# Attention and a cosine feed-forward on one core: weights decoded in pairs, the first tile cut in two around the second, and the start laid out by due times

## The chip, the core and the metric

The kernel runs on one core of a Trainium2 chip. TensorE (PE) multiplies, ScalarE (ACT) and VectorE (DVE) work on elements, GpSimd (POOL) does a few odd jobs, SyncE (SP) issues the DMAs. The metric is device time of one execution in microseconds (us); lower is better.

## What is computed

```
# q, k: random normals of about 0.573, v: 0.1; each (8, 8, 576, 64)
scores = scale * matmul(q_c, k_c^T)        # blocks of 64 positions, 9 in a sequence
attn = exp(scores - max); attn /= sum + 1e-9
x = matmul(attn, v_c)  ->  (4608, 512)     # heads side by side
h = x @ w_in                               # (512, 2048)
out = (h * cos(h)) @ w_out                 # (2048, 512)
```

The weights arrive as 64-bit floats and are decoded to 32-bit floats on the chip. Each large product is made in three passes of a fast 32-bit type: every operand is split in a rounded part ("hi") and the rest ("lo"), and hi x hi, hi x lo and lo x hi are added up.

## The kernel before

The 4608 tokens are 9 tiles of 512. w_in and w_out are cut along the 2048 inner columns in 16 blocks of 128 each; `("in", fc)` and `("out", fc)` name them. The kernel goes through 9 x 16 steps. In step s of tile t, `hidden(t, fc)` multiplies the tile's x with block fc of w_in (12 matmuls of 128x512 into PSUM bank h), `activate` makes g = h cos(h) from it in six instructions that go to and fro between ACT and DVE (whole turns on ACT, what is over on DVE, sine on ACT, product with h on DVE, g_hi on ACT, g_lo on DVE), and `project`, three steps behind (`LAG = 3`), adds g times block fc of w_out to four PSUM banks acc0 to acc3 (12 matmuls again). After a tile's last block the four banks are copied out (`finish`) and stored. There are two banks for h, so `hidden` of step s + 2 waits until the product with h of step s is done.

Attention of the next tile is made during a tile: `scores`, maximum, difference, exponential, sum, inverse, quotient, a transposition and `weighted`, whose result is split in the hi and lo parts of x. On PE these are four groups for a tile (two of scores, two of weighted values), two head pairs hp at a time. For tile 0 all of it comes before the first step; for tile 1 it is done in tile 0's steps in another form (`attend_early`), with the quotients on POOL.

Weights: `load_weight` brings a block of 512 KB to a room `w_in0`, `w_out0` and so on. `split_weight` decodes it. A double's upper 16 bits go into "half words" (magnitude: Abs; scale: Relu with factor 8, both on ACT; sign: or-ed in on DVE), its next 32 bits into a tile w (low: Relu on ACT), xor on DVE puts the two together, high (a copy on ACT) rounds, and rest (subtraction on DVE) gives the lo part. The lines from magnitude to xor, in this order magnitude, scale, low, sign, xor:

```
            half, low = half_words[(name == "out")], w.bitcast(U32)
            hb = half[:, :, 1]
            nc.scalar.activation(hb.bitcast(BF16), top.bitcast(BF16), AF.Abs)
            nc.scalar.activation(hb, hb, AF.Relu, bias=float(7 - (MORE << 7)), scale=8.0)
            nc.scalar.activation(low, mid, AF.Relu, bias=float((1 << 19) - 1), scale=-(2.0**-13))
            nc.vector.scalar_tensor_tensor(
                hb, top, 0x8000, hb, op0=ALU.bitwise_and, op1=ALU.bitwise_or
            )
            nc.vector.tensor_tensor(
                low, low, half.rearrange("p n k -> p (n k)").bitcast(U32), op=ALU.bitwise_xor
            )
```

So w_in blocks and w_out blocks each have a room of half words of their own (`half0`, `half1`). Two blocks of each kind are decoded ahead (`AHEAD = 2`).

Order: the instructions of tile 0's steps and of everything ahead of them are put in order on each engine by the framework's scheduler; from tile 1 on `keep_in_program_order` holds each engine to the order of the code, in which the queues `soon`, `late` and `full` place attention pieces behind parts of `activate`. Every engine works through its own instructions in order.

## Time and profile before

| | |
|---|---|
| time, median of 3 runs | 880.68 us (880.52 to 880.91) |
| time of the profiled execution | 880.95 us |
| its span, first to last instruction | 879.1 us |
| PE busy | 853.0 us (97%) |
| weight loads of PE (PEld) | 697.1 us (79%) |
| DVE busy | 576.7 us (66%) |
| ACT busy | 407.9 us (46%) |
| POOL busy | 5.5 us (1%) |
| moved by DMA | 55.42 MB, 63 GB/s over the span |

The profile is one execution on the chip. Busy shares are means over stages with different limits, so they are read by stretches of time; matmuls are pipelined, and a PE that is "busy" need not be at its best pace. The granted clock of TensorE has two levels, 1.2 GHz (0.50) and 2.4 GHz (1.00).

### The profile page before, as it was taken

The numbers are of one execution on the slowest core, as the hardware profiler recorded it, in microseconds if no ns is written. First come the engines' busy times: TensorE is split into PE (matmuls) and PEld (weight loads), VectorE is DVE, ScalarE is ACT, GpSimd is POOL, SyncE is SP. The second block draws the span as 40 slices with busy tenths as digits, with TensorE's granted clock in tenths as the row PEclk, the third lists the DMA queues.
The fourth block names the chain that finished last, engine by engine and source line by source line (L and its number), as shares of the span: only waits on it lengthen the run. The fifth ranks groups of instructions, "written<-read, shape, count | busy, mean of one in ns | idle before, by whom it ended". The sixth has DMA issues, their size and how long they took to land.

```text
span 879.1 us, 14100 instructions
## 1 busy us (share of the span) xinstructions
PE 853.0 (97%) x5792; PEld 697.1 (79%) x5792; DVE 576.7 (66%) x975; ACT 407.9 (46%) x660; POOL 5.5 (1%) x9
## 2 busy tenths in 40 slices
PE   4899999999999999999999999999999999999998
PEld 3587777888888888888888888888888888888886
DVE  5999986766577656764686558655766577644332
ACT  4998993533354335333533344333533354333332
POOL 0001000000000000000000000000000000000000
PEclk8599999999999999999999999999999999999999
DMA  9980013100310012001300040003100010001001
GB/s 346 406 340 33 14 25 110 47 26 25 96 49 25 24 49 96 25 1 50 120 1 25 25 145 1 25 25 97 49 25 25 1 48 25 1 1 48 1 1 48
DMA packets 25407, 55.42 MB, mean 63 GB/s; under 512 B 2816, under 2 KB 2816, under 8 KB 25344
## 3 DMA queue, kind: packets, MB, share of 16 engines
q1 hardware_dynamic: 25344, 54.54, 17.7%
q8 instruction: 45, 0.74, 0.4%
q14 instruction: 18, 0.15, 0.1%
HBM read 45.09 MB, written 9.44 MB: 62 GB/s over the span
## 4 chain that ended last, share of the span: by engine, by line
PE 85%; ACT 11%; DMA 1%; DVE 1%; issue 1%; SPq 0%; ACTq 0%
PE acc L74 41%; PE h L74 40%; PE a L74 4%; ACT half L124 2%; ACT half L125 2%; ACT w L126 2%; DMA w_out<-in_w_out_dram 1%; ACT g_hi L360 1%; ACT g L356 1%; ACT w_out L136 1%; ACT w_in L136 1%; ACT g L353 1%; DMA kt<-in_kT_dram 1%; ACT pts L270 0%; ACT x L321 0%
## 5 line engine op out<-in xcount | busy, mean ns | idle before, releaser
L74 PE MATMUL h<-x,w_in 128*128 128x512 f32 x1704 | 416.9, 393 | 5.9 <-ACT x L321 2.8
L74 PEld LDWEIGHTS h<-x,w_in 128*128 128x128 f32 x1704 | 321.1, 189 | 75.0 <-DVE g L357 4.5
L74 PE MATMUL acc<-w_out,g_hi 128*128 128x512 f32 x1152 | 355.2, 392 | 0.0
L74 PEld LDWEIGHTS acc<-w_out,g_hi 128*128 128x128 f32 x1152 | 214.0, 188 | 45.2
L74 PE MATMUL acc<-w_out,g_lo 128*128 128x512 f32 x576 | 221.1, 390 | 0.6 <-DVE g_lo L361 0.6
L354 DVE SCALAR_TENSOR_TENSOR g<-g,h 128x512 f32<-128x512 int32 x142 | 97.2, 684 | 138.3 <-ACT g L353 137.6
L353 ACT ACTIVATE g<-h 128x512 int32<-128x512 f32 x142 | 84.7, 596 | 190.1 <-PE h L74 190.1
L361 DVE TENSOR_TENSOR g_lo<-g,g_hi 128x512 fp32r<-128x512 f32 x144 | 102.5, 712 | 79.9 <-ACT g_hi L360 77.0
L356 ACT ACTIVATE g<-g 128x512 f32<-128x512 f32 x144 | 91.0, 632 | 128.2 <-DVE g L354 128.0
L360 ACT CAST g_hi<-g 128x512 fp32r<-128x512 f32 x144 | 89.3, 620 | 128.9 <-DVE g L357 79.3
L357 DVE TENSOR_TENSOR g<-h,g 128x512 f32<-128x512 f32 x142 | 98.1, 691 | 56.5 <-ACT g L356 53.0
L74 PEld LDWEIGHTS acc<-w_out,g_lo 128*128 128x128 f32 x576 | 108.1, 188 | 23.7 <-DVE g_lo L361 1.1
L282 DVE STREAM_TRANSPOSE pts<-e 32x256 f32<-32x256 f32 x224 | 97.4, 435 | 3.7
L125 ACT ACTIVATE half<-half 128x512 uint16<-128x512 uint16 x32 | 25.1, 786 | 0.2
L74 PEld LDWEIGHTS a<-kt,qt 64*64 64x64 f32 x1024 | 18.9, 135 | 7.6 <-issue 6.8
L130 DVE TENSOR_TENSOR w<-w,half 128x512 uint32<-128x512 uint32 x32 | 22.0, 687 | 1.8 <-ACT w L126 1.0
L74 PEld LDWEIGHTS a<-pts,vt 64*64 64x64 f32 x1024 | 16.6, 134 | 7.2 <-issue 5.3
L322 DVE TENSOR_TENSOR x<-a,x 128x512 fp32r<-128x512 f32 (+1 forms) x38 | 21.9, 614 | 0.1
L74 PE MATMUL a<-kt,qt 64*64 64x64 f32 x1024 | 21.8, 222 | 0.0
L74 PE MATMUL a<-pts,vt 64*64 64x64 f32 x1024 | 19.0, 222 | 0.7 <-ACT pts L270 0.7
L216 DVE TENSOR_TENSOR e<-a,m 128x512 f32<-128x512 f32 x28 | 19.2, 686 | 0.5
L212 DVE TENSOR_REDUCE m<-a 128x8 f32<-128x512 f32 x28 | 19.2, 684 | 0.0
(61 smaller groups left out, 316.5 us busy)
## 6 DMA issues: line engine op xcount, KB each, us to landing
qt<-in_qT_dram SPq DMA_DIRECT2D x36, 256.0 KB, 4.0
kt<-in_kT_dram SPq DMA_DIRECT2D x36, 256.0 KB, 4.2
vt<-in_v_dram SPq DMA_DIRECT2D x34, 256.0 KB, 3.0
w_in<-in_w_in_dram SPq DMA_DIRECT2D x16, 512.0 KB, 9.1
w_out<-in_w_out_dram SPq DMA_DIRECT2D x16, 512.0 KB, 9.4
out_dram<-w SPq DMA_DIRECT2D x16, 256.0 KB, 2.1
out_dram<-half SPq DMA_DIRECT2D x16, 256.0 KB, 2.0
out_dram<-x SPq DMA_DIRECT2D x4, 256.0 KB, 2.0
```

The lines of the kernel that those rows point to most:

```text
L74: kept(nc.tensor.matmul(*args, **kw))
L125: nc.scalar.activation(hb, hb, AF.Relu, bias=float(7 - (MORE << 7)), scale=8.0)
L130: nc.vector.tensor_tensor(low, low, half.rearrange("p n k -> p (n k)").bitcast(U32), op=ALU.bitwise_xor)
L212: kept(nc.vector.tensor_reduce(out=m, in_=sv, op=ALU.max, axis=AX.X))
L282: kept(nc.vector.transpose(out=dst[o : o + BL, :, qb], in_=src[i : i + BL, :, kb]))
L322: kept(nc.vector.tensor_tensor(lo, xq, hi.bitcast(F32), op=ALU.subtract))
L353: kept(nc.scalar.activation(n, h, AF.Identity, bias=0.25, scale=0.5 / math.pi))
L354: kept(nc.vector.scalar_tensor_tensor(g, n, -2.0 * math.pi, h, op0=ALU.mult, op1=ALU.add))
L356: kept(nc.scalar.activation(g, g, AF.Sin, bias=0.5 * math.pi))
L357: kept(nc.vector.tensor_tensor(g, h, g, op=ALU.mult))
L360: kept(nc.scalar.copy(out=g_hi, in_=g))
L361: kept(nc.vector.tensor_tensor(g_lo, g, g_hi.bitcast(F32), op=ALU.subtract))
```

## The change

Weights are loaded and decoded as pairs. A pair has one room of raw data, one tile w, and both its blocks pass each decoding instruction together (128x1024 elements instead of 128x512). There is one room of half words, for a pair, in place of two for a block. The pairs are, for the first eight and then for the last eight fc: (in, in) twice, (in, out) four times, (out, out) twice.

The order of steps is a list: tile 0 with fc 0 to 7, all of tile 1, tile 0 with fc 8 to 15, then tiles 2 to 8. The sums of tile 0's first half are copied from PSUM, stored to a DRAM buffer, and loaded again when tile 1 is out; DVE adds them to the second half's. Tile 2's attention falls in the second half of those first 32 steps (`STAGE`); its x take over tile 1's rooms (`x_room`, two sets of four, by parity).

All instructions are now held in program order. For the first 32 steps that order is made by the kernel: everything that one engine does is a piece (engine, length, what to run, pieces it comes after, time of a load), each piece gets a due time, going backwards from hidden and project blocks that follow each other from 23 us on, and a loop places next the piece that can start, by due time among those that can start within 0.2 us. Lengths in this list are constants of the source. Tile 1's four quotients and two of tile 0's are on POOL, one head pair at a time; exponentials of later tiles are two instructions of 1024 elements instead of one of 2048.

```diff
-    xp = ctx.enter_context(tc.tile_pool(name="xp", bufs=8))
+    xp = ctx.enter_context(tc.tile_pool(name="xp", bufs=4))
...
+    hbm = ctx.enter_context(tc.tile_pool(name="hbm", bufs=1, space=bass.MemoryType.DRAM))
...
-    ordered = False
-
     def kept(ins):
-        if ordered:
-            tc.keep_in_program_order(ins)
+        tc.keep_in_program_order(ins)
         return ins
...
-    half_words = []
-    for i in range(2):
-        half = wts.tile([P, TOK, 2], U16, name=f"half{i}")
...
+    half = wts.tile([P, 2, TOK, 2], U16, name="half")
...
+    def split_weights(pair):
...
+            pieces = [
+                lambda: kept(nc.scalar.activation(hb.bitcast(BF16), top.bitcast(BF16), AF.Abs)),
+                lambda: kept(nc.scalar.activation(hb, hb, AF.Relu, bias=more, scale=8.0)),
+                lambda: kept(nc.scalar.activation(
+                    w().bitcast(U32), mid, AF.Relu, bias=most, scale=-(2.0**-13)
+                )),
+                lambda: kept(nc.vector.scalar_tensor_tensor(
+                    hb, top, 0x8000, hb, op0=ALU.bitwise_and, op1=ALU.bitwise_or
+                )),
+                lambda: kept(nc.vector.tensor_tensor(
+                    w().bitcast(U32), w().bitcast(U32), words, op=ALU.bitwise_xor
+                )),
+            ]
...
+        def high():
+            parts = wts.tile([P, ROOM], F32R, name="w_%s%d_%s%d" % (*pair[0], *pair[1]))
+            made_parts.append(parts)
+            kept(nc.scalar.copy(out=beside(parts, at[0]), in_=w()))
...
+        def rest():
+            hi, lo = (beside(made_parts[0], at[0] + i * n) for i in range(2))
+            kept(nc.vector.tensor_tensor(lo, w(), hi.bitcast(F32), op=ALU.subtract))
...
+    def x_room(t, dtype):
+
+        return xp.tile([P, 2, TOK], dtype, name=f"x{(t + (t > 1)) % 2}")
...
+    order = [(0, fc) for fc in range(GROUP)] + [(1, fc) for fc in range(NFC)]
+    order += [(t, fc) for t in range(NT) if t != 1 for fc in range(0 if t else GROUP, NFC)]
...
+        if not whole:
+
+            os, to = att.tile([P, DM], F32, name="vt" if sub % 2 else "pts"), partial[sub]
+        elif t == 0:
+            os = acc["partial", sub]
...
+        if whole and t == 0:
+            kept(nc.vector.tensor_tensor(os, os, o, op=ALU.add))
...
+    for pair in pairs:
+        key = ("w", pair)
+        made[key] = split_weights(pair)
+        a = piece(ACT, 1.15, rest_of(key, 0), xored, at=here[pair])
+        r = piece(ACT, 1.15, rest_of(key, 1), a)
+        m = piece(ACT, 0.88, rest_of(key, 2), back[-2], at=here[pair])
+        g = piece(DVE, 1.19, rest_of(key, 3), r)
+        xored = piece(DVE, 1.13, rest_of(key, 4), m, g)
+        h = piece(ACT, 0.88, rest_of(key, 5), xored)
+        back.append(piece(DVE, 1.13, rest_of(key, 6), h))
...
+                if t or hp < 2:
+                    q[hp] = piece(POOL, 1.0, lambda hp=hp: quotient(t, hp, nc.gpsimd), i)
+                else:
+                    q[hp] = piece(DVE, 0.6, lambda hp=hp: quotient(t, hp), i)
...
+    for i in reversed(range(len(work))):
+        for a in work[i][3]:
+            due_at[a] = min(due_at[a], due_at[i] - work[a][5])
...
+                near = [
+                    (d if e != PE or work[i][1] > 2 else 0.0, start, i)
+                    for start, d, i in c if start <= soonest + 0.2
+                ]
+                d, start, i = min(near)
...
+    for start, i in sorted(starts):
+        work[i][2]()
+    for s in range(STAGE, len(order) + LAG):
...
```

Two places of the order on the engines show what the pairs do. The first is ACT in the middle of decoding. Before, in tile 0's steps (names end in buffer numbers; half0 and half1 are the two rooms of half words; L124 is the magnitude, L125 scale, L126 low, L136 high, L353 and L356 whole turns and sine, L360 g_hi):

```order
L136 CAST w_in5_710<-w_704 128x512
L124 ACTIVATE half0_87<-w_in6_158 128x512
L125 ACTIVATE half0_87<-half0_87 128x512
L360 CAST g_hi_534<-g_533 128x512
L353 ACTIVATE g_593<-a0_580 128x512
L126 ACTIVATE w_756<-w_in6_158 128x512
L136 CAST w_out5_719<-w_713 128x512
L124 ACTIVATE half1_89<-w_out6_160 128x512
L125 ACTIVATE half1_89<-half1_89 128x512
L356 ACTIVATE g_593<-g_593 128x512
```

After, around the pairs (in4, out0) and (in5, out1) (L136 is the magnitude, L137 scale, L138 low, L161 high, L388, L390 and L392 belong to the activation):

```order
L161 CAST w_in4_out0_573<-w_470 128x2x512
L136 ACTIVATE half_89<-w_in5_out1_143 128x1024
L137 ACTIVATE half_89<-half_89 128x1024
L388 ACTIVATE g_595<-h_548 128x512
L392 CAST g_hi_562<-g_561 128x512
L138 ACTIVATE w_618<-w_in6_out2_146 128x1024
L390 ACTIVATE g_595<-g_595 128x512
L161 CAST w_in5_out1_631<-w_567 128x2x512
L136 ACTIVATE half_89<-w_in6_out2_146 128x1024
L137 ACTIVATE half_89<-half_89 128x1024
```

Before, the magnitude of out6 goes to the other room right after that of in6; after, each magnitude stands behind the high of the pair before it and writes the same room `half_89`.

The second place is DVE at the same stretch. Before (L127 sign, L130 xor, L137 rest, L354, L357 and L361 the activation):

```order
L130 TENSOR_TENSOR w_756<-w_756,half0_87 128x512
L137 TENSOR_TENSOR w_out5_719<-w_713,w_out5_719 128x512
L127 SCALAR_TENSOR_TENSOR half1_89<-w_out6_160,half1_89 128x512
L357 TENSOR_TENSOR g_593<-a0_580,g_593 128x512
L354 SCALAR_TENSOR_TENSOR g_653<-g_653,a1_640 128x512
L137 TENSOR_TENSOR w_in6_762<-w_756,w_in6_762 128x512
L130 TENSOR_TENSOR w_765<-w_765,half1_89 128x512
L127 SCALAR_TENSOR_TENSOR half0_87<-w_in7_162,half0_87 128x512
L361 TENSOR_TENSOR g_lo_595<-g_593,g_hi_594 128x512
L357 TENSOR_TENSOR g_653<-a1_640,g_653 128x512
L130 TENSOR_TENSOR w_841<-w_841,half0_87 128x512
```

After (L141 sign, L144 xor, L168 rest, L389, L391 and L393 the activation, L277 to L282 sums and inverse of tile 1):

```order
L141 SCALAR_TENSOR_TENSOR half_89<-w_in4_out0_140,half_89 128x1024
L389 SCALAR_TENSOR_TENSOR g_561<-g_561,h_522 128x512
L144 TENSOR_TENSOR w_470<-w_470,half_89 128x1024
L391 TENSOR_TENSOR g_561<-h_522,g_561 128x512
L393 TENSOR_TENSOR g_lo_498<-g_496,g_hi_497 128x512
L168 TENSOR_TENSOR w_in4_out0_573<-w_470,w_in4_out0_573 128x2x512
L277 TENSOR_REDUCE z_546<-e0_429 128x8
L281 TENSOR_SCALAR z_546<-z_546 128x16
L282 RECIPROCAL z_546<-z_546 128x16
L141 SCALAR_TENSOR_TENSOR half_89<-w_in5_out1_143,half_89 128x1024
L389 SCALAR_TENSOR_TENSOR g_595<-g_595,h_548 128x512
L144 TENSOR_TENSOR w_567<-w_567,half_89 128x1024
```

Between a pair's sign and its xor there is now one instruction of the activation each time, and the next sign comes behind the pair's rest and, here, the inverses that POOL's quotients wait for.

## Rows read from the trace of the kernel before

**Rows 1.** Busy time of the engines by stretch of time (us from the span's start): length of the stretch; busy us of PE, PEld, DVE, ACT, POOL with their instructions; granted clock of TensorE, share of the DMA engines, GB/s.

```profile
40.00:80.00 40.00, 40.00 (x251) 32.83 (x252) 37.73 (x60) 39.66 (x64) 0.00 (x0) 0.96 0.64 245
...
80.00:127.00 47.00, 43.65 (x278) 34.00 (x277) 43.32 (x68) 44.79 (x83) 3.89 (x1) 1.00 0.05 12
...
160.00:800.00 640.00, 640.00 (x4338) 526.25 (x4337) 417.18 (x718) 252.42 (x396) 0.00 (x0) 1.00 0.12 39
```

**Rows 2.** The chain of waits (start, length, what): pieces of the steady part, and the end. h is a hidden block, acc a project block, a an attention group.

```profile
147.65 2.72 PE h L74 x12
...
211.53 1.09 PE a L74 x64
...
212.62 2.95 PE acc L74 x12
...
303.85 1.09 PE a L74 x64
...
864.69 10.89 PE acc L74 x48
```

**Rows 3.** Groups of instructions by line and shape, from 0 to 150 us: out<-in, shape, count | busy us, mean ns of one | idle before, and what ended it.

```profile
L124 ACT ACTIVATE half<-w_in 128x512 bf16<-128x512 bf16 x16 | 12.8, 802 | 2.2 <-DMA w_in<-in_w_in_dram 2.2
...
L125 ACT ACTIVATE half<-half 128x512 uint16<-128x512 uint16 x32 | 25.1, 786 | 0.2
...
L126 ACT ACTIVATE w<-w_out 128x512 uint32<-128x512 uint32 x16 | 10.6, 663 | 0.0
...
L136 ACT CAST w_in<-w 128x512 fp32r<-128x512 f32 x16 | 10.0, 624 | 0.0
...
L127 DVE SCALAR_TENSOR_TENSOR half<-w_in,half 128x512 uint16<-128x512 uint16 x16 | 12.0, 750 | 2.6 <-ACT half L125 2.6
...
L130 DVE TENSOR_TENSOR w<-w,half 128x512 uint32<-128x512 uint32 x32 | 22.0, 687 | 1.8 <-ACT w L126 1.0
...
L137 DVE TENSOR_TENSOR w_in<-w,w_in 128x512 fp32r<-128x512 f32 x16 | 11.0, 684 | 0.2 <-ACT w_in L136 0.2
...
L353 ACT ACTIVATE g<-h 128x512 int32<-128x512 f32 x16 | 9.5, 595 | 4.3 <-PE h L74 4.3
...
L356 ACT ACTIVATE g<-g 128x512 f32<-128x512 f32 x18 | 11.3, 625 | 2.4 <-DVE g L354 2.4
...
L360 ACT CAST g_hi<-g 128x512 fp32r<-128x512 f32 x18 | 11.1, 616 | 5.1 <-PE acc L74 3.5 <-DVE g L357 1.5
```

**Rows 4.** The timeline of all engines near 55 us: start, length, instruction, and in brackets the idle time ahead and what ended it.

```profile
54.83 0.79 ACT L124 ACTIVATE half<-w_out 128x512 bf16<-128x512 bf16 x1
...
55.65 0.79 ACT L125 ACTIVATE half<-half 128x512 uint16<-128x512 uint16 x1
...
56.30 0.61 ACT L356 ACTIVATE g<-g 128x512 f32<-128x512 f32 x1
...
56.47 0.77 DVE L127 SCALAR_TENSOR_TENSOR half<-w_out,half 128x512 uint16<-128x512 uint16 x1 [0.40 <-ACT half L125]
```

**Rows 5.** The page's DMA issues: count, KB each, median us from issue to landing.

```profile
out_dram<-w SPq DMA_DIRECT2D x16, 256.0 KB, 2.1
```

**Rows 6.** Groups by line and shape from 200 to 800 us (columns as in rows 3): g_lo, and a copy of a sum out of PSUM.

```profile
L361 DVE TENSOR_TENSOR g_lo<-g,g_hi 128x512 fp32r<-128x512 f32 x104 | 72.1, 693 | 63.1 <-ACT g_hi L360 60.6
...
L391 DVE COPY half<-acc 128x512 f32<-128x512 f32 x14 | 9.6, 682 | 0.0
```

**Rows 7.** The same view from 0 to 150 us: one instruction in two lengths on ACT and on DVE, and the load of a function table.

```profile
L224 ACT ACTIVATE e<-e 128x512 f32<-128x512 f32 x4 | 2.4, 609 | 5.8 <-DVE e L187 5.8
...
L224 ACT ACTIVATE e<-e 128x2048 f32<-128x2048 f32 x1 | 1.9, 1918 | 0.0
...
L227 DVE TENSOR_REDUCE z<-e 128x8 f32<-128x512 f32 x4 | 2.7, 680 | 0.8 <-ACT e L224 0.7
...
L227 DVE TENSOR_REDUCE z<-e 128x32 f32<-128x2048 f32 x1 | 2.3, 2286 | 0.6 <-ACT e L224 0.6
...
L356 ACT ACT_TABLE_LOAD x2 | 2.6, 1283 | 0.0
```

**Rows 8.** ACT's timeline: the first magnitude.

```profile
10.59 0.78 ACT L124 ACTIVATE half<-w_in 128x512 bf16<-128x512 bf16 x1 [2.16 <-DMA w_in<-in_w_in_dram]
```

**Rows 9.** Stretches of 2 us, columns as in rows 1.

```profile
30.00:32.00 2.00, 2.00 (x35) 1.69 (x34) 1.77 (x4) 2.00 (x5) 0.00 (x0) 0.50 1.04 409
...
38.00:40.00 2.00, 2.00 (x12) 1.22 (x12) 1.80 (x4) 1.97 (x5) 0.00 (x0) 0.50 1.02 401
```

**Rows 10.** PE's timeline: five matmuls of a hidden block, and 32 records of tile 1's scores.

```profile
30.88 2.34 PE L74 MATMUL h<-x,w_in 128*128 128x512 f32 x5
...
44.28 1.15 PE L74 MATMUL a<-kt,qt 64*64 64x64 f32 x32
```

**Rows 11.** The timeline of all engines around POOL's quotient of tile 1.

```profile
82.81 3.89 POOL L232 TENSOR_TENSOR e<-e,z 128x2048 f32<-128x2048 f32 x1 [80.63 <-ACT w L126]
...
83.14 0.68 DVE L354 SCALAR_TENSOR_TENSOR g<-g,h 128x512 f32<-128x512 int32 x1
...
83.73 3.52 DVE L361 TENSOR_TENSOR g_lo<-g,g_hi 128x512 fp32r<-128x512 f32 x1
...
87.31 0.96 PE L74 MATMUL acc<-w_out,g_lo 128*128 128x512 f32 x3 [0.64 <-DVE g_lo L361]
```

**Rows 12.** Waits from 0 to 150 us: who waited for whom: us in total, times, longest.

```profile
DVE half L127 <- ACT half L125: 4.0, 8, 1.3
```

More of the change, by code (lines that the diff above doesn't have):

```diff
@@ new lines, in load_weights @@
+    def load_weights(pair):
+        raw = wts.tile([P, 2 * ROOM if wide else ROOM], U16 if wide else F32, name="w_%s%d_%s%d" % (*pair[0], *pair[1]))
+        w_raw[pair] = raw
+        for i, (name, fc) in enumerate(pair):
+            src = w_in[:, fc].rearrange("p c f -> p (c f)") if name == "in" else w_out[:, fc]
+            n = src.shape[1]
+            if wide:
+                o = 1 + i * (4 * n + 2)
+                nc.sync.dma_start(out=raw[:, o : o + 4 * n], in_=src.bitcast(U16))
+            else:
+                nc.sync.dma_start(out=raw[:, i * n : i * n + n], in_=src)
@@ L234, in exponentials @@
[L234 to L256 removed]
+            found.extend((largest, below))
@@ new lines, in scores, with exponentials, total @@
+        return found
+    def exponentials(t, *hps):
+        for e in [weights_of(t, hp // 2)[:, hp % 2] for hp in hps] or [weights_of(t, g) for g in range(2)]:
+            e = e.rearrange("p c k -> p (c k)" if hps else "p a c k -> p (a c k)")
+            kept(nc.scalar.activation(e, e, AF.Exp, scale=SCALE))
+    sums = {}
+    def total(t, hp):
+        if hp == 0:
+            sums[t] = att.tile([P, HP, NCH], F32, name="z", bufs=1)
+        kept(nc.vector.tensor_reduce(out=sums[t][:, hp], in_=weights_of(t, hp // 2)[:, hp % 2], op=ALU.add, axis=AX.X))
@@ L309, in weighted @@
         if (t, g) not in x_parts:
-            x_parts[t, g] = tuple(
-                xp.tile([P, 2, TOK], F32R, name="x") for _ in range(2)
-            )
+            x_parts[t, g] = tuple(x_room(t, F32R) for _ in range(2))
+        splits = []
         for par in range(2):
@@ L391, in finish, with resume @@
             kept(nc.vector.tensor_copy(os, o))
[L392 to L406 removed]
+        nc.sync.dma_start(out=to, in_=os)
+    def resume():
+        for sub in range(NSUB):
+            os = acc["partial", sub] = out_room(sub)
+            nc.sync.dma_start(out=os, in_=partial[sub])
     pieces = {}
@@ L420, in attend @@
         if step == 3:
-            pieces["quotients"] = divide(t)
-        soon.extend(pieces["quotients"][a] for a in {4: (0, 1), 5: (2,), 6: (3,)}.get(step, ()))
+            soon.extend(lambda hp=hp: total(t, hp) for hp in range(HP))
+            soon.append(lambda: inverse(t))
+        for hp in {4: (0, 1), 5: (2,), 6: (3,)}.get(step, ()):
+            soon.append(lambda hp=hp: quotient(t, hp))
         if 4 <= step < 8 or 9 <= step < 13:
@@ L457, in attention_then_cos_ffn, with piece, loaded @@
-    for fc in range(AHEAD):
-        split_weight("in", fc)
-        split_weight("out", fc)
-    for s in range(NT * NFC + LAG):
-        t, fc = divmod(s, NFC)
-        ordered = t > 0
-        if t < NT:
+    PE, ACT, DVE, POOL, SP = range(5)
+    work = []
+    def piece(eng, length, run, *after, at=0.0, lag=0.15):
+        work.append([eng, length, run, [a for a in after if a is not None], at, length + lag])
+        return len(work) - 1
+    arrival = [3.6]
+    def loaded(mb, load, *args):
+        arrival[0] += 2.6 * mb
+        load(*args)
+        return arrival[0]
@@ new lines, in attention_then_cos_ffn, with made_by, go, rest_of @@
+    made = {}
+    def made_by(key, run, *args):
+        def go():
+            made[key] = run(*args)
+        return go
+    def rest_of(key, i):
+        return lambda: made[key][i]()
+    STAGE = 2 * NFC
+    split = {}
+    xored = None
+    back = [None, None]
+    for pair in pairs:
[8 more added lines that the diff above has]
+        back.append(piece(DVE, 1.13, rest_of(key, 6), h))
+        for block in pair:
+            split[block] = back[-1]
```

498 lines of the change are left out of this document (340 added, 158 removed).

## Prediction

> **What bounds the kernel now.** I read the stages first: the busy time of each engine in stretches [rows 1]. From 160 to 800 us PE is busy for 640.00 of 640 us at a granted clock of 1.00, while ACT has 252 and DVE 417. There the kernel is bound by PE alone. Before 127 us it is the other way round: from 40 to 80 us ACT is busy for 39.66 of 40 and DVE for 37.73, and from 80 to 127 us ACT for 44.79 of 47. PE is "busy" there too, but its matmuls get through far fewer blocks.
>
> The chain of waits puts numbers on the PE-bound part [rows 2]. A hidden or a project block is one piece of 2.72 us. An attention group costs 1.09 us and makes the next project block 2.95 instead of 2.72, so 1.32 us. Two such groups one tile apart stand at 211.53 and 303.85: 92.32 us, which is 32 x 2.72 + 4 x 1.32 (87.04 + 5.28). Nothing is lost there. From the hidden block at 147.65 (the 19th) 126 hidden and 129 project blocks and 26 groups are left: 255 x 2.72 + 26 x 1.32 = 727.9, which ends at 875.57. The trace has the last project piece end at 864.69 + 10.89 = 875.58. The span is 879.1, so the last copy and store are a tail of 3.5.
>
> So everything that can be won lies before the steady part. I measure it at one point: T8, the time at which the ninth hidden block starts, counted as if nothing stalled behind it. In the changed kernel 136 hidden blocks, 139 project blocks and the 28 attention groups of tiles 2 to 8 follow it: 275 x 2.72 + 28 x 1.32 + 3.5 = 788.5 us. On that scale the kernel before has T8 = 879.1 - 788.5 = 90.6. The profiled execution is 880.95, 1.85 over its span and 0.27 over the median; I add 1.85 to every span and compare with 880.68.
>
> **Who holds PE back before 127 us.** Each of the 32 weight blocks passes ACT four times and DVE three times [rows 3]: 802 (magnitude), 786 (scale), about 665 (low) and 623 ns (high) on ACT, 750 (sign), 687 (xor) and 685 ns (rest) on DVE. That is 2.88 us of ACT for a block, 92 us in all, or somewhat less since instructions that do not wait overlap: the scale at 55.65 lasts 0.79, and the next row starts at 56.30 [rows 4]. All blocks have to come before tile 0 is done, with 16 activations of 1.84 us each on ACT. Tile 0 is due at once and uses every block for the first time, so PE waits for ACT.
>
> **The change, part by part.**
>
> *Half of the weights first.* Tile 0 needs only 8 + 8 blocks in its first half, and then tile 1 goes over the same 8 + 8 for another 8 steps. The first 8 pairs become urgent, and the other 8 have 8 steps of 5.44 us more (43.5 us) and get off the path: 7 pairs at about 4.3 us of ACT and 9 activations at 1.5 are 44 us against 49 of PE. What it adds is four copies of partial sums (two on ACT, two on DVE), four stores, four loads, and four adds on DVE in place of two copies there and two on ACT. The loads have some 16 steps (87 us) between store and use, against a landing time of 2.1 us for a store [rows 5]; the copies and adds (0.68 us for one on DVE [rows 6]) fall where ACT and DVE have room. I cost all of it at nothing; without the cover it would be 4 x 0.7 + 2 x 2 = 7 us at most.
>
> *Two blocks in one instruction.* No row has 1024 elements. From below: 128x512 and 128x2048 take 609 and 1918 ns on ACT, 680 and 2286 on DVE [rows 7], so 512 more elements cost 0.436 and 0.535. That gives 1.24 for the magnitude and scale, 1.06 for high, 1.28 for sign, 1.22 for xor. From above: twice the single length, 1.60, 1.57, 1.25, 1.50, 1.37. The magnitude and scale are dearer than other 512-element rows, and whether that part comes once per instruction or per element no row tells; for these two I take the middle between 1.24 and 1.43 (twice, less one fixed part of 0.17), 1.33, and for the others the lower ends, as they resemble the rows of the line.
>
> *One room for the half words.* This is the step that decides. Before, blocks of w_in and w_out had a room of half words each, so one block could be on ACT while the other was on DVE. Now a pair has one room, and the order on ACT and DVE makes a ring of each pair: magnitude, scale (ACT), sign, a turn of the activation, xor (DVE), high (ACT), and only then the next magnitude, which overwrites the half words that xor read. Hand-overs cost some 0.03 us: the scale at 55.65 ends at 56.44 and DVE's sign starts at 56.47; a dependent pair on ACT is 0.82 apart at a length of 0.79 [rows 4]. The ring: 1.33 + 1.33 + 1.20 (sign, overlapping its successor) + 0.60 (turn) + 1.22 + 0.95 (high, overlapping) + 0.1 = 6.7 us. The lower lengths give 6.5, the double ones 8.0. PE wants a pair each 5.44 us (one hidden, one project), so the ring and not PE sets the pace until tile 1's x are ready. For two of the pairs ACT has more between scale and high (x casts of 0.25 to 0.5, copies, activations), and it is ACT's sum: 7.2.
>
> *The start.* The first block is on ACT at 10.59, when its transfer has landed [rows 8]; the pair's second 0.52 MB at 409 GB/s [rows 9] comes at 11.9. From there I follow the order on each engine with these lengths. ACT: magnitude of the first pair to 13.2, an exponential, scale to 15.0, an exponential, two copies of transposed weights to 16.3, low to 17.3, four x casts to 18.8 (they wait for PE at half clock), two copies to 21.1. DVE: sign 15.0 to 16.2, sums, inverse and two quotients to 18.3, x parts, xor to 20.7, two more x parts. So high of the first pair runs at 21.1 to 22.0 and its rest to 23.3; the weighted values of the last two head pairs, 1.13 us each on PE, give the last x of tile 0 at 24.9. The first hidden block goes from 25 to 29. PE's clock is granted at 0.50 (1.2 of 2.4 GHz) from 30 to 32 us before, and again from 38 to 40 [rows 9], where a matmul takes 0.47 us (five in 2.34 [rows 10]) instead of 0.227; I give the first block 1.3 us for that. Then two scores of tile 1 (1.15 us each [rows 10]) to 31.2, DVE's differences to 33.0, the exponentials to 33.7, the table load of 1.28 [rows 7] and the first sine to 35.5, scale of the third pair to 36.8, sign 38.1, turn 38.7, xor 39.9, high 41.3 (ACT's work alone, 13 two-block instructions for 14.0, 25 smaller ones and a table load for 10.6, would end at 36.5; the difference is waits, most of them for PE and DVE ahead of the first hidden block's end). With that pair project 0 can run.
>
> *POOL takes tile 1's quotients.* Before it was one instruction of 3.89 us at 82.81, and beside it DVE's g_lo took 3.52 instead of 0.69 [rows 6, 11]: 2.83 us lost, 0.73 of POOL's time, and PE waited 0.64 for it. A turn (one input in PSUM) at 83.14 was not held. Now it is four instructions of about 0.97, in two couples, each at a time when sign and xor, both with two SBUF inputs, are part of the ring. By the row: 0.73 x 3.89 = 2.8 us. The Trainium skill, "SBUF — State Buffer", section "Who interferes with whom", says that a DVE instruction with two SBUF inputs contends with a GpSimd one that reads SBUF, and that the loser blocks for the whole instruction; by that the four could take up to 3.9 us, 1.1 more than by the row. Tile 0's two quotients on POOL run while DVE reads PSUM; nothing.
>
> *Sum.* 41.3 + 3 x 6.7 + 2 x 7.2 + 2.8 = 78.6 for high of the eighth pair. On ACT follow a sine, a g_hi and two x casts of 128x512 (2.1), then DVE's last x (0.6): 81.3. The ninth hidden block needs them at its eighth matmul, 1.6 after its start: T8 = 79.7. 79.7 + 788.5 + 1.85 = 870.0 us, 10.7 or 1.2% less than before.
>
> Other parts cost nothing: exponentials as two of 1024 (0.17 more on ACT, which is under 40% busy after 160 us), and the rooms of x by parity, where tile 2's casts wait once for tile 1's last hidden block, with activations behind them that have three steps of slack.
>
> **Rivals.**
> 1. *PE keeps up.* T8 is then 25 + 13 x 2.72 + 1.3 + tile 1's attention (about 7) = 68.7, or 859 us. It needs the ring to hide, which its lower end (6.5 against 5.44) speaks against; with every low length and POOL harmless the sum is T8 = 75.4, or 865.7. Below 865: chance 0.17.
> 2. *Forecast*, 865 to 875: 0.60.
> 3. *Two blocks cost twice one.* Five rings of 8.0 and 2 us more at the start: T8 = 88.2, 878.5. For it: the dear 2-byte rows; against: the line from 512 to 2048. 875 to 879: 0.15.
> 4. *No change*, 879 to 882.4: the end of rival 3 with one more wait. 0.04.
> 5. *Slower.* Engines run in order, so each of the hand-overs scale to sign and xor to high can find the other engine in an unrelated instruction. Before, DVE waited 8 times, 4.0 us in all, for scale alone [rows 12]. The sum bears 10.7 us; over five rings that is 2.1 each, so from a ring of 8.8 on the kernel is slower: two foreign instructions of 1 us per ring. At 9.3 it is 883. Nothing in the order puts so many there: 0.04.
>
> **How the numbers follow.** 0.2% (1.8 us) is about what a measurement of this kernel can tell from no change. Faster is rivals 1 to 3, 0.92; same 0.04; slower 0.04. The range 862 to 878 leaves out the half of rival 1 that comes near 859 and the top of rival 3 and beyond, some 0.18.
>
> **What would show it.** In the profile after, the steady part must keep 92.32 us per tile and 2.72 per block. Until about 80 us the chain should run through ACT and DVE in turns, with a magnitude about each 6.7 us, PE idle for one to two us in each, and DVE the releaser. Two-block rows should be 1.25 to 1.4 (magnitude, scale), 1.06 (high) and 1.2 to 1.3 on DVE. Two or three DVE rows beside POOL's should be longer by 0.7 us or so. After 82 us PE should hardly stop. I am wrong if ring and magnitudes come at 5.4 us, if the first hidden block starts away from 25, or if PE stops after its ninth hidden block: for late weights of the second half, for partial sums, or where tile 2's attention waits in PE's order.

## The result, and the profile after

The changed kernel takes 889.73 us (median of 4 runs, 887.65 to 889.95) against 880.69: a ratio of 1.0097, with a 95% interval of 1.0080 to 1.0115. I had forecast 870.0 and a range of 862 to 878. The sign was wrong as well as the size. The profiled execution is 889.62 at a span of 887.8, so what lies around the span is 1.8 as before, and 19.6 us have to be found inside it. In experiment 3, and in the first kernel of experiments 11 and 12, one run of five took about 1720 us, twice the time of the others; the medians below leave it out (877.40 and 876.53 us), while the recorded expectations quote them with it (877.84 and 877.23).

The stages first, as in [rows 1].

```profile
40.00:80.00 40.00, 35.38 (x275) 27.62 (x274) 35.90 (x46) 37.23 (x46) 6.34 (x4) 1.00 0.68 263
80.00:127.00 47.00, 44.91 (x250) 35.28 (x249) 38.10 (x45) 40.97 (x51) 0.00 (x0) 1.00 0.12 41
127.00:160.00 33.00, 30.88 (x185) 24.76 (x184) 27.44 (x40) 23.23 (x30) 0.00 (x0) 0.95 0.16 55
160.00:800.00 640.00, 640.00 (x4294) 517.64 (x4293) 410.32 (x709) 249.08 (x393) 0.00 (x0) 1.00 0.12 41
```

The last row is the one to stop at. PE is busy for 640.00 of 640 us at a granted clock of 1.00, as before, but gets through 4294 records where it had 4338. Nothing waits there; PE itself is slower. The chain in the steady part, as in [rows 2]:

```profile
421.95 1.09 PE a L71 x64
...
426.03 2.75 PE h L71 x12
428.78 2.80 PE acc L71 x12
...
442.67 2.72 PE h L71 x12
445.39 2.80 PE acc L71 x12
448.19 2.78 PE h L71 x12
...
456.45 2.73 PE acc L71 x12
...
515.71 1.09 PE a L71 x64
```

Blocks took 2.72 us each before. Now they take 2.72 to 2.80, and which ones are long repeats from tile to tile. Two groups one tile apart stand at 421.95 and 515.71: 93.76 us instead of 92.32.

The other loss is in PE's timeline. These are the rows in which it stops for more than 0.3 us behind the eighth hidden block, with the group ahead of them, and then two pieces of the chain and the clock at that place.

```profile
77.97 1.16 PE L71 MATMUL a<-pts,vt 64*64 64x64 f32 x64
...
81.97 0.49 PE L71 MATMUL h<-x,w_in_in 128*128 128x512 f32 x1 [1.24 <-ACT x L351]
83.02 1.43 PE L71 MATMUL h<-x,w_in_in 128*128 128x512 f32 x5 [0.56 <-DVE x L354]
...
138.88 1.16 PE L71 MATMUL a<-kt,qt 64*64 64x64 f32 x62 [2.09 <-DVE e L261]
```

```profile
140.04 4.53 PE acc L71 x12
144.57 2.75 PE h L71 x12
```

```profile
140.00:144.00 4.00, 4.00 (x13) 3.15 (x12) 4.00 (x6) 1.88 (x3) 0.00 (x0) 0.57 0.79 257
```

The ninth hidden block is in its eighth matmul at 83.02, which makes T8 = 83.02 - 7 x 0.227 = 81.4; it waits for tile 1's last x, made from the group at 77.97. Then PE stands for 2.09 us at tile 2's second scores, and the projection behind them, at a granted clock of 0.57 (for most of it the lower level), takes 4.53 us.

The two-block rows (0 to 150 us, as in [rows 3]) came out near the forecast:

```profile
L136 ACT ACTIVATE half<-w_in_out 128x1024 bf16<-128x1024 bf16 x8 | 11.0, 1380 | 0.0
L137 ACT ACTIVATE half<-half 128x1024 uint16<-128x1024 uint16 x16 | 21.7, 1359 | 0.3
L138 ACT ACTIVATE w<-w_in_out 128x1024 uint32<-128x1024 uint32 x8 | 9.2, 1151 | 0.0
L161 ACT CAST w_in_out<-w 128x1024 fp32r<-128x1024 f32 x8 | 8.4, 1051 | 4.0 <-DVE w L144 3.9
L141 DVE SCALAR_TENSOR_TENSOR half<-w_in_in,half 128x1024 uint16<-128x1024 uint16 x4 | 5.5, 1366 | 2.5 <-ACT half L137 2.4
L168 DVE TENSOR_TENSOR w_in_out<-w,w_in_out 128x1024 fp32r<-128x1024 f32 x8 | 9.8, 1220 | 1.0 <-ACT w_in_out L161 1.0
```

### The profile page after: what moved, and what is told of

Read it like the earlier page. It is cut to its first block, busy times and chain, and to the rows that moved or that the text cites. A ratio compares the mean times of both kernels' runs of the same rounds, so it can differ in the third digit from the quotient of the medians.

```text
span 887.8 us, 14013 instructions
## 1 busy us (share of the span) xinstructions
PE 861.7 (97%) x5792; PEld 695.9 (78%) x5792; DVE 571.3 (64%) x926; ACT 405.1 (46%) x600; POOL 10.0 (1%) x13
## 3 DMA queue, kind: packets, MB, share of 16 engines
q1 hardware_dynamic: 26496, 56.63, 17.8%
## 4 chain that ended last, share of the span: by engine, by line
PE 84%; DMA 6%; ACT 5%; DVE 3%; issue 1%; SPq 0%; ACTq 0%; DVEq 0%
PE acc L71 42%; PE h L71 39%; PE a L71 3%; DMA w_in_out<-in_w_in_dram 3%; DMA qt<-in_qT_dram 2%; ACT half L137 1%; ACT half L136 1%; DMA w_in_in<-in_w_in_dram 1%; DVE w L144 1%; DVE half L141 1%; DMA kt<-in_kT_dram 1%; DVE g L389 0%; ACT w_in_out L161 0%; ACT g_hi L392 0%; DVE g_lo L393 0%
## 5 line engine op out<-in xcount | busy, mean ns | idle before, releaser
L71 PE MATMUL h<-x,w_in_in 128*128 128x512 f32 x864 | 212.8, 394 | 5.3 <-DVE g L391 3.5
L71 PE MATMUL h<-x,w_in_out 128*128 128x512 f32 x864 | 210.6, 392 | 3.4 <-DVE g L391 3.4
L71 PEld LDWEIGHTS h<-x,w_in_in 128*128 128x128 f32 x864 | 161.7, 188 | 44.3 <-DVE g L391 4.4
L71 PEld LDWEIGHTS h<-x,w_in_out 128*128 128x128 f32 x864 | 161.6, 187 | 40.8 <-DVE g L391 4.6
L389 DVE SCALAR_TENSOR_TENSOR g<-g,h 128x512 f32<-128x512 int32 x144 | 98.5, 684 | 146.2 <-ACT g L388 145.6
L71 PE MATMUL acc<-w_out_out,g_hi 128*128 128x512 f32 x576 | 182.7, 398 | 0.0
L388 ACT ACTIVATE g<-h 128x512 int32<-128x512 f32 x144 | 85.8, 596 | 210.3 <-PE h L71 210.1
L71 PE MATMUL acc<-w_in_out,g_hi 128*128 128x512 f32 x576 | 181.0, 395 | 0.3 <-ACT pts L452 0.3
L393 DVE TENSOR_TENSOR g_lo<-g,g_hi 128x512 fp32r<-128x512 f32 x144 | 99.3, 691 | 75.1 <-ACT g_hi L392 71.9
L392 ACT CAST g_hi<-g 128x512 fp32r<-128x512 f32 x144 | 89.2, 620 | 124.9 <-DVE g L391 80.5
L390 ACT ACTIVATE g<-g 128x512 f32<-128x512 f32 x144 | 90.9, 632 | 115.8 <-DVE g L389 115.2
L391 DVE TENSOR_TENSOR g<-h,g 128x512 f32<-128x512 f32 x144 | 99.5, 691 | 56.2 <-ACT g L390 53.1
L71 PEld LDWEIGHTS acc<-w_in_out,g_hi 128*128 128x128 f32 x576 | 107.5, 188 | 26.0 <-ACT pts L452 0.7
L71 PEld LDWEIGHTS acc<-w_out_out,g_hi 128*128 128x128 f32 x576 | 107.3, 189 | 24.6
L71 PE MATMUL acc<-w_out_out,g_lo 128*128 128x512 f32 x288 | 114.0, 396 | 0.0
L71 PE MATMUL acc<-w_in_out,g_lo 128*128 128x512 f32 x288 | 112.9, 392 | 0.0
L71 PEld LDWEIGHTS a<-kt,qt 64*64 64x64 f32 x1024 | 19.6, 138 | 11.0 <-issue 7.3
L277 DVE TENSOR_REDUCE z<-e 128x8 f32<-128x512 f32 x36 | 23.7, 677 | 1.7 <-ACT e L270 1.7
```

The source lines that it names most:

```text
L71: kept(nc.tensor.matmul(*args, **kw))
L277: kept(nc.vector.tensor_reduce(out=sums[t][:, hp], in_=weights_of(t, hp // 2)[:, hp % 2], op=ALU.add, axis=AX.X))
L388: lambda: kept(nc.scalar.activation(n, h, AF.Identity, bias=0.25, scale=0.5 / math.pi)),
L389: lambda: kept(nc.vector.scalar_tensor_tensor(g, n, -2.0 * math.pi, h, op0=turns, op1=over)),
L390: lambda: kept(nc.scalar.activation(g, g, AF.Sin, bias=0.5 * math.pi)),
L391: lambda: kept(nc.vector.tensor_tensor(g, h, g, op=ALU.mult)),
```

## What could make a matmul longer

The operands' places in SBUF were moved by the change, which I had not counted as an edit. They follow from the code. Each of these matmuls has a loaded operand of 128 columns (PEld's rows) and a moving one of 512: in a hidden block the block of w_in is loaded and x moves, in a projection g is loaded and the block of w_out moves. Before, a block's room was 2 x 512 + 32 floats, 4224 bytes; the blocks of w_in had every second room, so that they stood 8448 = 33 x 256 bytes apart, and those of w_out as well. A room for a pair is 2080 floats, 8320 = 32.5 x 256 bytes, so every second pair stands 128 bytes off modulo 256. The rooms of x and g are multiples of 256 bytes and all begin alike. Take the start of the moving operand less the start of the loaded one (called weights from here on, g included), modulo 256 bytes. Before, this difference is 16 for all 1728 matmuls of hidden blocks (the 112 bytes of SHIFT are the reason) and 0 for all 1728 of projections. After, it is 16 and 144 for half of the hidden ones each, and 0 and 128 for half of the projections each. In the trace the hidden blocks with 144 start a matmul every 233.0 ns on average, those with 16 every 227.4.

**Theory A**: the place of one operand against the other sets PE's pace. **Rival B**: the pace is lost to the double-width rooms, to the two rings of x, or to what ACT and DVE do meanwhile.

## Experiments on the place of the operands

**1. The kernel before, x and g 128 bytes later.**

```
+    gap = ctx.enter_context(tc.tile_pool(name="gap", bufs=1))
+    nc.gpsimd.memset(gap.tile([P, 32], F32, name="gap"), 0.0)
     xp = ctx.enter_context(tc.tile_pool(name="xp", bufs=8))
```

> The kernel before with 128 bytes per partition that nobody reads, allocated between the weights' side and the pools of x and g, so that every x and g room begins 128 bytes later and nothing else moves. Theory A (TensorE's pace depends on whether the moving operand and the weights that are loaded next lie in the same 128-byte half of a 256-byte line): before, the start addresses of the pairs differ by 0 or 16 bytes modulo 256 in all 3456 large matmuls, here by 128 or 144; in the kernel after, the hidden blocks with 144 start a matmul every 233.0 ns and those with 16 every 227.4 ns. So all blocks go from 2.72 to about 2.80 us, a tile from 92.32 to about 94.8, and the run takes 900 to 903 us (275 blocks by 0.078 more than 880.7). Rival B (the pace is lost to the double-width rooms, the two x rings, or to what VectorE and ScalarE read meanwhile): nothing of that is in this kernel, so 880.7 within 0.2%, blocks 2.72.

Measured: 898.94 us (898.64 to 899.70), a ratio of 1.0202 (1.0186 to 1.0217). The chain:

```profile
420.48 1.09 PE a L76 x64
...
424.56 2.79 PE h L76 x12
...
434.21 2.80 PE acc L76 x12
...
515.01 1.09 PE a L76 x64
```

128 bytes that nobody reads cost 17.8 us. Every block is long, and a tile takes 94.53 us. So A's cost exists, and none of B's causes is in this kernel; whether B has a share in the kernel after, experiment 3 tells. The total is 1 to 4 us under what I expected, as hidden blocks went to 2.78 and 2.79 and not to 2.80.

**2. The kernel before, SHIFT 32.**

```
-SHIFT = 28
+SHIFT = 32
```

> The kernel before with SHIFT 32 in place of 28: the hidden blocks' weights begin 16 bytes later, so that x and weights differ by 0 bytes modulo 256 instead of 16 (the projection's have 0 already). Theory A in its plain form (only the 128-byte half matters): 880.7 us within 0.2%, blocks 2.72. Theory A with a second part (the 16 bytes put the two streams into step at the change of block): each block pays the settling that projections show in the kernel after, 234, 236, 224, 231, 236, 229, 232, 231 and then 227 ns, 0.037 us a block, so 275 blocks give up to 891 us. Rival B: 880.7.

Measured: 880.84 us, a ratio of 0.9998 (0.9989 to 1.0008); all blocks 2.72. A difference of 0 is as good as one of 16, and the second part of the theory is not needed. It also corrects my wording: with SHIFT 28 the weights begin at 240 and x at 0 modulo 256, in different halves of a 256-byte line, and that is fast. It is the difference that counts, not the half.

**3. The kernel after, all operands at one place.** Blocks begin at 0 in every second room and at 32 floats in the others.

```
-        at = [SHIFT if name == "in" else 0 for name, _ in pair]
-        step = 2 * n + at[1] - at[0]
-        if pair[0][0] != pair[1][0]:
-            step += 32
+        at = [32 * odd] * 2
+        step = 2 * n
```

> The kernel after with one thing changed, where the decoded blocks lie in their rooms: blocks at 0 and 1024 floats in every second room and at 32 and 1056 in the others, so that all weights, x and g begin at 128 modulo 256 bytes (difference 0 in all 3456 large matmuls; in the kernel after it is 16 or 0 in half of them and 144 or 128 in the other half). The double-width rooms, the two x rings, the operations and their order stay. Theory A: a tile falls from 93.76 to 92.32 us, and the run by 275 blocks by 0.045, to 876 to 878 us; if the difference of 0 in hidden blocks costs a settling (the second part), 878 to 887. Rival B: 889.7 within 0.3%, blocks as uneven as in the kernel after.

Measured: 877.40 us, 0.9958 of the kernel before (0.9943 to 0.9972). 12.3 us come back, and the change is now a small gain. The profile of the kernel of experiment 6, which has the same places, shows the blocks:

```profile
417.49 1.09 PE a L71 x64
...
421.53 2.72 PE h L71 x12
424.25 2.72 PE acc L71 x12
...
509.81 1.09 PE a L71 x64
```

A tile takes 92.32 us again, with the double-width rooms and the two rings of x in place: B has no share that could be seen.

**4. The kernel after, x and g 128 bytes earlier.** The four small rooms m move from ahead of x and g to behind them (a pool of their own).

> The kernel after with its four small rooms of maxima (128 bytes together) allocated behind x and g instead of ahead of them, so that all x and g rooms begin 128 bytes earlier. Theory A: slow and fast blocks change places: hidden blocks 0, 1, 4, 6, 8, 9, 12, 14 of a tile (2.78 to 2.80 us in the kernel after) fall to 2.72 to 2.75, and 2, 3, 5, 7, 10, 11, 13, 15 (2.72 to 2.75) rise to 2.78 to 2.80; the time stays at 888 to 891 us, as half of the blocks are on the wrong side either way. Rival B (it is the rooms or what runs beside a block): the same blocks stay slow.

Measured: 889.99 us in one run. At the place in the tile that the rows of after show above:

```profile
426.20 2.79 PE h L72 x12
...
448.38 2.72 PE h L72 x12
...
456.68 2.80 PE acc L72 x12
```

The hidden block of 2.75 at 426.03 is one of 2.79 here, the one of 2.78 at 448.19 is one of 2.72, and the projection of 2.73 at 456.45 is one of 2.80. Slow and fast have changed places. So it is the place of neither operand by itself: in the kernel after, x begins alike in all blocks and the weights' rooms decide; here the weights are where they were and the move of x turns the outcome round. (The time tells nothing, since half of the blocks are wrong either way.)

**5. The kernel before, x and g 64 bytes later.** As experiment 1, with 16 floats for 32.

> The kernel before with 64 unused bytes per partition between the weights' side and the pools of x and g (128 of them gave 898.94 us, and 2.80 us a block). Start addresses of moving operand and next weights differ here by 80 bytes modulo 256 in hidden blocks and by 192 in projections. If the cost grows step by step with the distance: about half of the loss for the hidden blocks, some 885 to 895 us. If there are only two cases, with the line between them somewhere between 16 and 128: each kind of block is either at 227 or at 233 ns a matmul. Rival (only a multiple of 128 matters): 880.7 us.

Measured: 894.54 us in one run.

```profile
429.60 2.76 PE h L76 x12
432.36 2.79 PE acc L76 x12
```

Hidden blocks (a difference of 80) take 2.76 us, between the 2.72 of 16 and the 2.78 of 144; projections (192) take 2.79, nearly the 2.80 of 128. The 2.76 is no leftover of the slow block ahead: within a hidden block the matmuls start 226, 229, 236 and 229 ns apart, over and over, and don't come down to 227. Not only a multiple of 128 matters, and it is no clean two cases either. How the cost runs between these points was not measured, and as 80 was had with x moving and 192 with w_out moving, the two are not compared on one kind of block.

## Experiments on the order

Places right, the kernel is at 877.4, while T8 = 81.4 would give 81.4 + 788.5 + 1.85 = 871.8. The rest had to be in PE's waits.

**6. Tile 2's second scores one projection later.**

```
-                below.append(piece(DVE, 0.6, rest_of(key, 2 * h + 1), m))
+                below.append(piece(DVE, 0.6, rest_of(key, 2 * h + 1), m, lag=2.0))
```

> The kernel with all operands at the same place modulo 256 bytes (877.84 us), and one number of the planner besides: it reckons 2 us more until tile 2's subtracted scores are out of their banks, so that TensorE's second group of scores for tile 2 stands behind one more projection (12 matmuls) in its order. Theory: in the kernel after, TensorE stands for 2.09 us at these scores, and the projection behind them runs at a granted clock of 0.66 in 140 to 145 us and takes 4.44 us instead of 2.75, so 3.8 us in all; the projection that now comes first covers the wait, and the time falls to 873.5 to 874.5 us. Rival: VectorE is late for the tile as a whole, and the wait only moves to the next group: 877 to 878 us.

Measured: 877.93 us, 0.9967 (0.9954 to 0.9980): nothing. PE's timeline:

```profile
158.12 3.03 PE L71 MATMUL h<-x,w_in_out 128*128 128x512 f32 x12 [1.27 <-DVE g L389]
...
173.82 0.69 PE L71 MATMUL a<-pts,vt 64*64 64x64 f32 x32 [1.52 <-DVE pts L311]
174.90 0.68 PE L71 MATMUL a<-pts,vt 64*64 64x64 f32 x28 [0.39 <-DVE pts L311]
```

```profile
84.00:88.00 4.00, 4.00 (x12) 3.14 (x11) 3.01 (x4) 2.82 (x4) 0.00 (x0) 0.57 0.02 4
```

The wait for the scores is gone, and PE waits later, for DVE, at a hidden block and at tile 2's weighted values. The rival was right in that the wait moved and the time stayed. In addition a clock of 0.57 now stands behind the waits at 80 to 83 us.

**7. The planner's costs set to the rows.** The order on each engine comes from a plan in which each piece has a cost. For the two-block pieces it reckoned 1.15 + 1.15 + 0.88 + 0.88 = 4.06 us of ACT for a pair, where the rows above have 1.38 + 1.36 + 1.15 + 1.05 = 4.94.

```
-        a = piece(ACT, 1.15, rest_of(key, 0), xored, at=here[pair])
+        a = piece(ACT, 1.39, rest_of(key, 0), xored, at=here[pair])
```

and so for scale (1.36), low (1.16), sign (1.38), xor (1.22), high (1.05), rest (1.22) and POOL's quotient (1.6). (The expectations of experiments 7 and 10 call the prediction's low, L138, "turn" and its rest, L168, "low".)

> The kernel with later scores, with the planner's costs of the double-width pieces set to the rows of the kernel after (magnitude 1.39, scale 1.36, turn 1.16, sign 1.38, exclusive or 1.22, high 1.05, low 1.22, GpSimd quotient 1.6; they stand at 1.15, 1.15, 0.88, 1.19, 1.13, 0.88, 1.13, 1.0). Theory A (the pairs come every 7.2 us instead of the predicted 6.7 because ScalarE's and VectorE's work for a pair adds up to that): the order hardly matters, and the time stays within 0.1% of the kernel with later scores. Theory B (the pieces queue up in an order made for shorter ones): the eight pairs are out up to 1.7 us earlier, and the time falls by 0.1 to 0.2%.

Measured: 867.25 us (866.94 to 867.66), 0.9840 (0.9826 to 0.9855). This is 10.7 us less than experiment 6, six times what the bolder theory gave it.

**8. The same without the 2 us of experiment 6.**

> The kernel with all operands at the same place modulo 256 bytes (877.84 us) with the eight costs set to the rows, without the 2 us that were added for tile 2's subtracted scores. Theory (the costs alone make the order; the two added microseconds, which gave nothing by themselves, do nothing here either): 866 to 869 us, the ninth hidden block at 77 us and no wait of TensorE at tile 2's attention. Rival (both are needed): 870 to 875 us, with a wait of about 2 us at tile 2's second scores.

Measured: 867.82 us, 0.9848 (0.9833 to 0.9863). The costs alone do it. Stages, and PE's and DVE's timelines around tile 1's last x:

```profile
80.00:127.00 47.00, 47.00 (x267) 38.80 (x266) 39.20 (x50) 40.41 (x52) 0.00 (x0) 1.00 0.17 56
127.00:160.00 33.00, 33.00 (x205) 27.18 (x204) 30.12 (x45) 25.22 (x32) 0.00 (x0) 1.00 0.11 33
```

```profile
70.54 1.16 PE L71 MATMUL a<-pts,vt 64*64 64x64 f32 x64
...
77.21 1.07 PE L71 MATMUL h<-x,w_in_in 128*128 128x512 f32 x4
```

```profile
73.40 1.28 DVE L352 TENSOR_TENSOR x<-a,x 128x512 fp32r<-128x512 f32 x2
```

In the kernel after, that x is DVE's row

```profile
81.69 1.27 DVE L354 TENSOR_TENSOR x<-a,x 128x512 fp32r<-128x512 f32 x2
```

With the longer costs the plan puts tile 1's last weighted group ahead of the eighth hidden block (70.54) instead of behind the projection that follows it (77.97). Tile 1's x is there 8 us earlier, the ninth hidden block starts at 77.21 without a wait, and from 80 us on PE is never idle. 77.2 + 788.5 = 865.7, against a span of 866.1: with places and order right, the sum from T8 holds. (The place of that group is not the only way to an early T8: in experiment 12 it stands behind the eighth hidden block and its projection again, at 74.68, and T8 is 76.7, as the magnitude of the eighth pair there comes 3.3 us earlier than in the kernel after, at 68.81 against 72.15.)

**9. The costs alone, places as in the kernel after.**

> The kernel after with the planner's eight costs set to its own rows, and nothing else (the operands stand as in the kernel after: half of the large matmuls at a difference of 128 or 144 bytes). Theory (the two losses, place of the operands and order, add up): the places cost 889.73 - 877.84 = 11.9 us, so 867.25 + 11.9 = 879.1, that is 878 to 880.5 us, with blocks of 2.72 to 2.80 and no wait of TensorE behind the first seven blocks of tile 1. Rival (with a slower TensorE the waits would have been covered anyway, or the order found for one is no good for the other): 883 to 889 us.

Measured: 880.19 us, 0.9983 (0.9974 to 0.9993). The four kernels, in us:

| | places as in after | one place |
|---|---|---|
| costs as in after | 889.73 | 877.40 |
| costs from the rows | 880.19 | 867.82 |

The places cost 12.3 and 12.4, the order 9.5 and 9.6. The two add up. (The kernel before, timed beside these runs, had medians from 880.69 to 881.64 us, so that half a us in such a difference tells nothing.)

**10. Costs from the steps between starts.**

> The kernel with measured costs, with the step from one instruction's start to the next one's in the engine's busy stretches taken for a cost instead of the row's own length (the rows overlap by about 0.1 us): magnitude 1.41, scale 1.23, turn 1.16, sign 1.26, exclusive or 1.14, high 0.96, low 1.14, GpSimd quotient 1.6. Theory A (costs near the rows are what the order needs, and small differences don't matter): 865 to 869 us. Theory B (which order the planner falls on is chance, and 867.25 was a lucky one): anywhere from 868 to 878 us.

Measured: 874.33 us, 0.9918 (0.9902 to 0.9935). In PE's waits from 80 to 200 us stands again

```profile
PE a L71 <- DVE pts L311: 1.9, 2, 1.5
```

Six costs that differ by 0.02 to 0.13 us (two are the same) give an order that loses 6.5 to 7 us of the 10: tile 1's last weighted group stands at 77.54, behind the eighth hidden block, as in the kernel after, T8 is 80.1, and behind the waits above a projection takes 4.22 us (granted clock 0.66 from 170 to 175 us). So theory B has a share. Experiments 7 to 9 are not three witnesses against it: they have the same eight costs, and 8 and 9 have the same order on every engine, as the plan knows costs and not places. Shown is that the order of the kernel after loses about 10 us against that one. That its costs are too short is the reason, and that costs near the rows give a good order as a rule, is not shown. Each order has to be measured.

**11 and 12. Tile 1's quotients on DVE instead of POOL**, in the kernels of experiments 6 and 7.

```
-                if t or hp < 2:
+                if t == 0 and hp < 2:
                     q[hp] = piece(POOL, 1.0, lambda hp=hp: quotient(t, hp, nc.gpsimd), i)
```

> The kernel with later scores, with tile 1's four quotients on VectorE (0.68 us each by the rows) instead of GpSimd. By my prediction GpSimd's four held VectorE up by 0.73 of their time; in the kernel after they take 1.6 us each, 6.34 us in all, and the VectorE rows beside them are longer by 0.69, 0.08 and 0.1 us, with 1.11 us idle ahead of one. Theory A (the price on record, 2.8 us, near what the quotients cost on VectorE itself): no difference to the kernel with later scores within 0.1%. Theory B (GpSimd holds VectorE up by the 0.9 us of the longer rows alone): VectorE gets 2.7 us of work for 0.9 us of relief, and the ninth hidden block starts up to 1.8 us later: 0.1 to 0.2% slower.

> The kernel with measured costs, with tile 1's four quotients on VectorE at 0.6 in the plan instead of GpSimd. With the old costs this gave 877.23 against 877.93 us, no difference that its intervals part. Theory A (GpSimd's work costs VectorE about as much as the quotients do themselves): 867.25 within 0.2%. Theory B (VectorE has no room: its busy share from 40 to 80 us is 94%): 869 to 871 us. If GpSimd's hold on VectorE is what still makes TensorE wait before 80 us: 864 to 866 us.

Measured: 876.53 us, 0.9942 (0.9926 to 0.9959), against 877.93; and 867.91, 0.9849 (0.9834 to 0.9864), against 867.25. Neither pair of intervals parts. For the kernel of experiment 7 the rows fit theory A: beside POOL's quotients four DVE rows are longer by 0.61, 0.81, 0.74 and 0.24, together 2.4 us, where the quotients would cost DVE itself 4 x 0.68 = 2.7. In the kernel of experiment 6, which keeps the order of the kernel after there, DVE loses half of that (see POOL below) and no difference shows either. But moving the quotients also gives another order, and an order can be worth several us, so that these runs put no sharp price on POOL's hold.

## Why the prediction was wrong, point by point

**The steady part (the step that failed).** "In the profile after, the steady part must keep 92.32 us per tile and 2.72 per block": I took 275 x 2.72 over to the new kernel because neither the matmuls nor their number change, and wrote that other parts cost nothing, the rooms of x by parity among them. But a block's length depends here on where its operands lie, and the change moved them. The term is mis-sized by 1.44 us per tile, 12.4 us over 275 / 32 = 8.6 tiles; the four kernels measure 12.3 and 12.4. Nothing in the trace of before could give this price, since there all differences were 0 or 16; but PAD = 32 and SHIFT = 28 in the source of before were the places to ask what they were for.

**T8.** 79.7 forecast, 81.4 measured: 1.7 us. This is the start: the first hidden block ran from 26.80 (25 forecast) and high of the third pair ended at 43.1 (41.3), 1.8 late. From there to high of the eighth pair, which ended at 79.92, it took 36.8 us, where I had 37.3. Magnitudes came at

```profile
50.84 1.38 ACT L136 ACTIVATE half<-w_in_out 128x1024 bf16<-128x1024 bf16 x1
...
72.15 1.39 ACT L136 ACTIVATE half<-w_out_out 128x1024 bf16<-128x1024 bf16 x1
```

so 21.31 / 3 = 7.1 us per pair, between the 6.7 of the ring and the 7.2 of ACT's sum. The two-block lengths were right to 0.05 us for magnitude, scale, high and rest; sign (1.37) was 0.09 longer. The question that I had left open has an answer, too: from 512 to 1024 elements the magnitude grew by 0.58 us and scale by 0.57, against 0.436 on the line from 512 to 2048, so what makes them dear comes for the most part per element. But the ring need not decide T8: experiment 8 has T8 = 77.2 although its last two magnitudes of the first half are 9.3 us apart (63.66 and 72.92), as its x come earlier. I followed the ring, and not where the order put the last weighted group.

**POOL.** 2.8 us forecast. POOL's two couples took 3.15 and 3.19 us, 1.6 for a quotient instead of 0.97:

```profile
45.62 3.15 POOL L287 TENSOR_TENSOR e<-e,z 128x512 f32<-128x512 f32 x2 [30.64 <-DVE z L282]
```

```profile
45.83 2.07 DVE L141 SCALAR_TENSOR_TENSOR half<-w_in_out,half 128x1024 uint16<-128x1024 uint16 x1 [0.38 <-ACT half L137]
...
48.38 1.46 DVE L144 TENSOR_TENSOR w<-w,half 128x1024 uint32<-128x1024 uint32 x1
```

Beside the first couple DVE lost 0.70 and 0.24 us, beside the second 0.28: 1.2 in all, under half of the forecast. (A sign stood idle for 1.11 us beside the second, but that was ACT: its scale ended at 60.50, and the sign began at 60.54.) The two held each other up by turns. In the row of 3.15 the first quotient runs for 1.05 us, to 46.67, and the second for 2.14, from 46.62 to 48.76. The sign starts under the first quotient and ends 1.23 after it, the second quotient starts under the sign and ends 0.86 after it, and the xor starts under the second quotient and ends 1.08 after it: each time a little less than the late one's own length (1.37, 1.05 and 1.22). By the rule of the Trainium skill ("SBUF — State Buffer", "Who interferes with whom"), which the prediction named, the loser blocks until the other's instruction is over; these rows agree with it, and the loser is whichever came second, in the second quotient of each couple POOL itself.

**Waits behind the ninth hidden block.** I had priced them at nothing and named "where tile 2's attention waits in PE's order" as what would make me wrong. It did: 2.09 us and 1.8 for the projection at a granted clock of 0.57. Together with T8 this is 5.6 us. Experiments 8 and 9 put the whole of the order at 9.5 and 9.6, since a good one also brings T8 under my forecast.

**The account.** 12.4 (pace) + 1.7 (T8) + 3.9 (scores and clock) = 18.0 of 19.6 us; 0.3 more is a wait for copies of partial sums, and 1.3 I can't assign.

**Rivals.** The slower one ended right in sign and wrong in its mechanism: from 43 to 72 us the magnitudes came 6.9 to 7.8 apart, and no ring took 9 us. That two blocks cost twice one fell with the rows (the magnitude 1.38 for 1.60); its sum was off besides, as five rings of 8.0 and 2 us more make T8 87.2 and 877.5 us, not 88.2 and 878.5. "PE keeps up" (859) did not come in any kernel. With places and order right the kernel is at 867.25, 2.75 us under the forecast and 1.6% under the kernel before: what the change removes can be worth about what I worked out, and what it moved took it back. That the two totals lie so near is partly luck: T8 is 77 there and not 79.7, by an order that I had not foreseen, and experiment 10 missed it with nearly the same costs.

## What to carry to other kernels

A change that moves rooms can change the pace of the matmuls that read them: compare the start of the moving operand with the start of the weights, modulo 256 bytes, before and after, and where a bound stage is "unchanged", look at the length of one block in the chain first. Where a plan's costs make the order of the engines, a change that makes pieces longer calls for new costs, and a wait that is moved in such an order can come back further on, as in experiment 6. Small steps in the costs moved the time by several us here, so that each order must be timed.

## What the runs showed of the hardware that I had not expected

- PE's pace depends on the places of its operands while PE is 100% busy at a granted clock of 1.00. For differences (moving operand less weights, modulo 256 bytes) of 0 and 16 a block of 12 matmuls of 512 columns takes 2.72 us, for 80 it takes 2.76, for 192 2.79, for 144 2.78 to 2.80, for 128 2.80. The busy share shows nothing of it.
- The pace also has a memory. In the kernel after, a projection with difference 0 that follows a slow hidden block takes 2.76 us, with 234, 236, 224, 231, 236, 229, 232 and 231 ns from start to start until it settles at 227; behind a fast hidden block it takes 2.73. A hidden block with difference 16 behind a slow projection takes 2.75 and does not settle within its 12 matmuls.
- Waits of about 1.25 and 0.56 us at 80 to 83 us were followed by a clock of 0.57 from 84 to 88 us in experiment 6 and by none in the kernel after, where they were as long and PE had been as busy (2.18 and 2.20 us of the 4 before 84). The projection behind them took 4.2 us in the one and 2.8 in the other. What parted the two is not shown.
